# Step 2's transposes on TensorE and its feed-forward in one piece, with wider planning margins

## The chip, the cores and the metric

One core of one Trainium2 chip runs the whole program. The number to explain is the device time of one launch in microseconds (us). Before the change the median of three executions is 214.18 us (212.68 to 214.71). The execution that was profiled took 214.71 us. Its span in the trace is 213.0 us, and the 1.7 us around it are not in the trace.

## The reference, cut to what matters

A gated linear attention runs over 4 batches, 8 heads, 768 positions and a head size of 48. Its output, 3072 rows of 384, goes through a feed-forward with 1536 inner rows.

```python
f = 1.0 / (1.0 + np.exp(-f_logit))
for t in range(S):
    state = f[:, :, t, :, None] * state + np.einsum('bhd,bhe->bhde', k[:, :, t], v[:, :, t])
    y[:, :, t] = np.einsum('bhd,bhde->bhe', q[:, :, t], state)
...
x = np.ascontiguousarray(attn_out.transpose(0, 2, 1, 3)).reshape(B * S, H * D)
...
gate = np.maximum(x @ w_gate, 0.0)
val = x @ w_val
return (gate * val @ w_out).astype(np.float32)
```

## The kernel before, in words

**Steps.** The 768 positions are cut into six steps (`c` = 0 to 5) of 128 positions. In every step each of the four batches (`b`) goes through `attention(c, b)`, and then 512 rows (4 batches of 128) go through the feed-forward of that step.

**Attention of one batch in one step.** ScalarE takes the exponential and the logarithm of the gate's logits for two batches at once (L576, L579). TensorE adds the logarithms up along the positions (the cumulative sums, L586 and L588), ScalarE exponentiates the result (L595, L597), and GpSimd multiplies k and q by it (L606, L609, into `hats`). These are then transposed into `qkT`: in steps 0 and 1 by TensorE into PSUM (L619) and copied out by VectorE (L625), from step `first_xbar_qk` on by a transposing DMA that SyncE's queue issues (L628). TensorE forms the scores (L642), VectorE masks them into `ptm` (L648, two instructions for a batch), TensorE forms the output (L677, L681), and ScalarE copies it to `xn` (L695). The output is transposed once more into `xT`, by TensorE and VectorE in steps 1 and 2 (L703, L707) and by a transposing DMA from step 3 on (L711). The state for the next step is made by L722, L736 and L738.

**Feed-forward.** For each of 12 blocks `j` of 128 inner rows, `ffn_hidden` (L754) forms the gate and the value, each with three matmuls over the columns of the batches `b0` to `b1`. ScalarE applies the relu (L761), VectorE multiplies (L765, into `gT`). `ffn_out` (L776) then forms one batch's output with 12 matmuls of 384 columns, ScalarE copies it to `osb` (L788) and SyncE's queue stores it (L791). The list `groups` says how the batches of a step are taken together: an entry `(2,0,2,0)` is step 2, batches 0 and 1 together, so matmuls of 256 columns; `(4,0,4,0)` is all four batches at once with 512 columns. An entry needs the `xT` of all its batches.

**What sets the order.** Nothing is ordered at run time. `Plan.schedule` gives every operation an estimated start from fixed costs (`occ`, `lat`, for a DMA also `flow` and `late`), always takes the operation that could start earliest, and writes one fixed order for each engine; each engine then runs its order and waits on semaphores where an operand comes from elsewhere. The planner adds a margin to the estimated arrival of an operand: `pl.margin` for TensorE and SyncE, and `pl.more` on top for TensorE operations of the attention once the planned time is past `pl.later` (85.0). Feed-forward matmuls have a priority number from 1000 up, take no margin, and serve as filler. PSUM has eight banks: two for scores, four for the feed-forward, one each for the rest.

**SyncE's queue.** Loads of f, k, q and v (L398; 384 KB each, two batches), transposing DMAs and stores all stand in one queue in the planned order. A load waits until the load three places before it has landed (`flight = 3`), and a transposing DMA or store waits for the engine that makes its operand. Whatever stands behind waits too.

Of the kernel before, what the change touches and what calls it, by code (L numbers as in the profile page):

```python
# [43 lines left out]
class Plan:  # L44
# [9 lines left out]
    def add(self, eng, emit, reads=(), writes=(), occ=0.5, lat=0.2, prio=0, opens=(), after=(), follows=(),  # L54
            paced=()):
        op = Op(eng, emit, list(reads), list(writes), occ, lat, prio, opens, after, follows, paced)
        op.idx = len(self.ops)
        self.ops.append(op)
        return op
# [169 lines left out]
def bass_hgrn2_outer__then__ffn_reglu_kernel(  # L229
# [11 lines left out]
             "q0.2.3 q0.3.4 v0.2.3 v0.3.4 wg0 wv0 wg1 wv1 wg2 wv2 wg3 wv3 f1.0.2 k1.0.2 q1.0.2 v1.0.2 "  # L241
             "wo0 wo1 wo2 f1.2.4 k1.2.4 q1.2.4 v1.2.4").split()
    lag = 4.0
    first_xbar_qk = 2
    flight = 3
    WP = 0
    NWARM = 100
# [6 lines left out]
    first_xbar_x = 3  # L254
    load_batches = 2
    hat_engines = ['DVE', 'POOL']
    groups = [(0,0,4,1),(1,0,2,0),(1,2,4,0),(2,0,2,0),(2,2,4,0),(3,0,2,0),(3,2,4,0),(4,0,4,0),(5,0,4,0)]
    B, H, S, D = q.shape
    C = 128
    NC = S // C  # L260
# [12 lines left out]
    NL = 3  # L273
# [42 lines left out]

    pl = Plan({"bc": 1, "tp": 1, "s": 2, "y": 1, "kv": 1, "f": 4, "w": 1})
    pl.settled, pl.margin = 40.0, {"PE": 0.5, "SP": 0.6}
    pl.later, pl.more = 85.0, 0.5
    add = pl.add  # L320
    gp, ve, sc, te, sy = nc.gpsimd, nc.vector, nc.scalar, nc.tensor, nc.sync

# [51 lines left out]
    def dma(op, slot, flow, late=0.8):  # L374

        if slot not in slots:
            slots[slot] = [nc.alloc_semaphore(f"d_{slot}"), 0]
        slots[slot][1] += 16
        op.sem, op.goal = slots[slot]
        op.flow, op.late = flow, late  # L380
# [3 lines left out]
    def load(n, c, b0, b1, after=(), paced=(), eng="SP"):  # L384
        last = tails.get("load" + eng)
        e = sy if eng == "SP" else sc
        t = ld[n][c % NL]
        src = bass.AP(tensor=srcs[n].tensor, offset=b0 * H * S * D + c * C * D,
                      ap=[[D, C], [S * D, (b1 - b0) * H], [1, D]])
        dst = t[:, b0:b1, :, :].rearrange("p b h d -> p (b h) d")  # L390
        flow = 0.9 * (b1 - b0)
        if c == 0 and n != "v":
            u = b0 % 2
            src = bass.AP(tensor=srcs[n].tensor, offset=b0 * H * S * D, ap=[[2 * D, 64], [S * D, H], [1, 2 * D]])
            dst = t[64 * u:64 * u + 64, b0 - u:b0 - u + 2, :, :].rearrange("p b h d -> p (b h d)").rearrange(
                "p (h x) -> p h x", h=H)
            flow = 0.82
        op = add(eng, lambda: e.dma_start(dst, src), [], [f"{n}{c % NL}_{b}" for b in range(b0, b1)],  # L398
                 occ=(0.6 if eng == "SP" else 0.3) * (b1 - b0) * (0.8 if c == 0 else 1), lat=2.0 if c == 0 else 0.9, prio=c * 100 - 150 * (eng != "SP"), after=after,
                 follows=[last] if last else [], paced=paced)  # L400
        tails["load" + eng] = op
        dma(op, f"{n}{c % NL}_{b0}{b1}", flow, (6.0 if (c, n, b0) == (1, "v", 0) else 2.0 if c < 3 else 2.0) if c else 0.8)
        return op

    w_cuts = {"wg": [int(x) for x in ['0', '2', '4', '8', '12']], "wo": [0, 4, 8, 12]}
# [7 lines left out]
    def load_w(nm, s, after, landed=()):  # L413
        j0, j1 = w_cuts[nm][s:s + 2]
        if nm == "wo":
            src = bass.AP(tensor=w_out.tensor, offset=j0 * 128 * DM, ap=[[DM, 128], [128 * DM, j1 - j0], [1, DM]])
            dst = wo[:, j0:j1, :]
        else:
            src = bass.AP(tensor=wsrc[nm].tensor, offset=j0 * 128,
                          ap=[[DFF, 128], [128 * DFF, NK], [1, (j1 - j0) * 128]])  # L420
            dst = (wg if nm == "wg" else wv)[:, :, j0 * 128:j1 * 128]
        last = tails.get("load_w")
        op = add("POOL", lambda: gp.dma_start(dst, src), [], [f"{nm}{s}"], occ=0.8, lat=1.0, prio=WP, paced=after,
                 after=landed, follows=[last] if last else [])
        tails["load_w"] = op
        dma(op, f"{nm}{s}", 6.3 * (j1 - j0) / NJ)
        return op
# [4 lines left out]
    for item in early:  # L432
        weight = item[0] == "w"
        cost, need = 0.0, []
        for other, flow, op in reversed(done):
            if cost >= lag and other != weight:
                need = [op]
                break
            cost += flow
        if weight:  # L440
            landed = [first_of[wo_after[int(item[2:])]]] if item[:2] == "wo" else []
            op = load_w(item[:2], int(item[2:]), [] if landed else need, landed)
        else:
            c, b0, b1 = (int(x) for x in item[1:].split("."))
            op = load(item[0], c, b0, b1, need)
            if c == 1:
                first_of.setdefault(item[0], op)
        done.append((weight, op.flow, op))
# [9 lines left out]
    for i in range(NWARM):  # L458
        op = add("PE", lambda: te.matmul(cold.ap[:, 0:256], zeros[:, 0:128], zeros[:, :]), ["zeros"], [cold], occ=0.22 if i < NCOLD else 0.11,  # L459
                 lat=PE_L, prio=1000000, opens=[cold] if i == 0 else [])  # L460
# [342 lines left out]
    for c in range(NC):  # L803
        for b in range(0, B, load_batches):
            for n in "fkqv":
                if c > max(int(x.split(".")[0]) for x in sent):
                    if load_engine == "SP":
                        loads.append(load(n, c, b, b + load_batches, loads[-flight:][:1]))
                    else:
                        loads.append(load(n, c, b, b + load_batches, paced=loads[-flight:][:1], eng="ACT"))  # L810
        for b in range(B):
            attention(c, b)
        if c == 0 and split_first:
            for j0 in range(0, NJ, JB):
                for b0 in (0, 2):
                    for j in range(j0, j0 + JB):
                        ffn_hidden(0, b0, b0 + 2, j)
            for b in range(0, B, OPAIR):
                ffn_out(0, *range(b, b + OPAIR))
        for gc, b0, b1, now in groups:  # L820
            if gc != c or (c == 0 and split_first):
                continue
            for j in range(NJ):
                ffn_hidden(c, b0, b1, j)
                if pend and (NJ - 1 - j) * 1.0 / NJ * len0 < len(pend):
                    ffn_out(*pend.pop(0))
            mine = [(c, b) for b in range(b0, b1)]
            pend = pend + mine
            while now and pend:
                ffn_out(*pend.pop(0))  # L830
            len0 = len(pend)
# [6 lines left out]
    for e in ("PE", "ACT", "DVE", "POOL"):  # L838
        n = 0
# [72 lines left out]
```

## Time and profile before

| | |
|---|---|
| median of three executions | 214.18 us |
| profiled execution / its span | 214.71 us / 213.0 us |
| TensorE busy | 191.2 us (90%), clock at 0.998 |
| ScalarE, VectorE, GpSimd busy | 117.5, 106.6, 78.8 us |
| feed-forward matmuls of 256 columns (L754) | 576, in groups of three |
| feed-forward matmuls of 512 columns (L754) | 144, in groups of three |
| transposing DMAs for `qkT` / for `xT` | 16 / 12 |
| last load issued | 145.38 us from the start |

In the profile, a line such as L628 is a line of the kernel above. "PE" is TensorE's matmuls, "PEld" its weight loads, "DVE" VectorE, "ACT" ScalarE, "POOL" GpSimd, and "SPq" SyncE's queue. Matmuls are pipelined, so the duration that the profile gives for one is longer than the distance between two starts; distances are what adds up. A group of three 256-column matmuls takes 0.49 us by itself, but the next group starts 0.33 us later.

### The profile page before, as it was taken

The numbers are of one execution on the slowest core, as the hardware profiler recorded it, in microseconds if no ns is written. First come the engines' busy times: TensorE is split into PE (matmuls) and PEld (weight loads), VectorE is DVE, ScalarE is ACT, GpSimd is POOL, SyncE is SP. The second block draws the span as 40 slices with busy tenths as digits, with TensorE's granted clock in tenths as the row PEclk, the third lists the DMA queues.
The fourth block names the chain that finished last, engine by engine and source line by source line (L and its number), as shares of the span: only waits on it lengthen the run. The fifth ranks groups of instructions, "written<-read, shape, count | busy, mean of one in ns | idle before, by whom it ended". The sixth has DMA issues, their size and how long they took to land.

```text
span 213.0 us, 4826 instructions
## 1 busy us (share of the span) xinstructions
PE 191.2 (90%) x1903; PEld 134.3 (63%) x1903; DVE 106.6 (50%) x228; ACT 117.5 (55%) x287; POOL 78.8 (37%) x113
## 2 busy tenths in 40 slices
PE   7896999979999999959768678788999999999994
PEld 6685788756886877737555556555775454445562
DVE  7248966444694767544545445334582535233310
ACT  2976758527898775928428457084454434433411
POOL 5389103913879737465642433606100000000000
PEclk9999999999999999999999999999999999999999
DMA  5999999999999999999999799899922010111112
GB/s 128 233 217 180 202 201 200 221 205 246 253 190 196 202 170 243 188 198 187 144 207 202 144 223 133 172 218 181 209 59 74 0 42 0 37 37 37 40 42 107
DMA packets 123207, 32.83 MB, mean 154 GB/s; under 512 B 115504, under 2 KB 123184, under 8 KB 123184
## 3 DMA queue, kind: packets, MB, share of 16 engines
q1 hardware_dynamic: 118400, 28.98, 70.7%
q0 software_dynamic: 4784, 3.54, 11.1%
q8 instruction: 15, 0.25, 0.5%
q14 instruction: 8, 0.07, 0.2%
HBM read 25.95 MB, written 4.72 MB: 144 GB/s over the span
## 4 chain that ended last, share of the span: by engine, by line
PE 55%; DMA 19%; SPq 12%; ACT 7%; POOL 3%; issue 2%; DVE 1%
PE ps L754 30%; PE ps L776 16%; SPq L398 5%; DMA f_in<-in_f_logit_dram 5%; DMA qkT<-hats 5%; SPq L628 5%; DMA wo<-in_moe_w_out_dram 3%; DMA v_in<-in_v_dram 3%; DMA q_in<-in_q_dram 3%; ACT relu L761 2%; PE ps L642 2%; SPq L711 2%; PE ps L722 1%; ACT f_in L576 1%; ACT bneg L579 1%
## 5 line engine op out<-in xcount | busy, mean ns | idle before, releaser
L765 DVE TENSOR_TENSOR gT<-relu,ps 128x256 bf16<-128x256 bf16 (+1 forms) x120 | 54.3, 470 | 58.5 <-ACT relu L761 29.5
L754 PE MATMUL ps<-xT,wv 128*128 128x256 bf16 (+1 forms) x360 | 66.7, 294 | 2.1 <-ACT relu L761 1.2
L761 ACT ACTIVATE relu<-ps 128x256 bf16<-128x256 f32 (+1 forms) x120 | 49.9, 429 | 31.9 <-PE ps L754 31.1
L754 PE MATMUL ps<-xT,wg 128*128 128x256 bf16 (+1 forms) x360 | 66.6, 294 | 0.4 <-DVE xT L707 0.4
L776 PE MATMUL ps<-wo,gT 128*128 128x384 bf16 x288 | 52.4, 326 | 1.3 <-DMA wo<-in_moe_w_out_dram 1.3
L754 PEld LDWEIGHTS ps<-xT,wv 128*128 128x128 bf16 x360 | 33.3, 98 | 14.7 <-ACT relu L761 1.4
L754 PEld LDWEIGHTS ps<-xT,wg 128*128 128x128 bf16 x360 | 33.6, 98 | 12.2 <-DVE xT L707 0.7
L648 DVE TENSOR_TENSOR ptm<-ps,tri 128x512 bf16<-128x512 f32 x48 | 31.0, 684 | 17.3 <-PE ps L642 17.2
L776 PEld LDWEIGHTS ps<-wo,gT 128*128 128x128 bf16 x288 | 26.7, 98 | 17.7 <-DMA wo<-in_moe_w_out_dram 1.7
L788 ACT ACTIVATE osb<-ps 128x384 f32<-128x384 f32 x24 | 11.6, 489 | 30.3 <-PE ps L776 30.2
L606 POOL TENSOR_TENSOR hats<-k_in,expo 128x384 bf16<-128x384 f32 x20 | 19.9, 997 | 16.7 <-ACT expo L595 16.6
L609 POOL TENSOR_TENSOR hats<-q_in,expo 128x384 bf16<-128x384 f32 x20 | 20.0, 998 | 10.1 <-DMA q_in<-in_q_dram 8.0
L738 POOL TENSOR_TENSOR st<-ssum,dec 128x384 bf16<-128x384 f32 x16 | 13.3, 830 | 17.2 <-DVE ssum L736 17.2
L642 PE MATMUL ps<-qkT 48*128 48x128 bf16 x192 | 9.5, 218 | 7.8 <-DMA qkT<-hats 7.8
L562 POOL CAST vpad<-v_in 128x384 bf16<-128x384 f32 x24 | 11.9, 518 | 11.0 <-DMA v_in<-in_v_dram 10.3
L576 ACT ACTIVATE f_in<-f_in 128x768 f32<-128x768 f32 x10 | 8.4, 841 | 13.4 <-DMA f_in<-in_f_logit_dram 13.4
L459 PE MATMUL ps<-zeros 128*128 128x256 bf16 x91 | 12.8, 294 | 1.1 <-DVE zeros L358 1.1
L695 ACT ACTIVATE xn<-ps 128x384 bf16<-128x384 f32 x20 | 9.8, 488 | 6.2 <-PE ps L681 6.1
L642 PEld LDWEIGHTS ps<-qkT 48*128 48x128 bf16 x192 | 5.5, 94 | 11.9 <-issue 6.6
L736 DVE TENSOR_TENSOR ssum<-ps,st 128x384 f32<-128x384 f32 x16 | 8.9, 554 | 6.9 <-PE ps L722 6.8
L595 ACT ACTIVATE expo<-ps 128x384 f32<-128x384 f32 x20 | 9.9, 496 | 2.3 <-PE ps L588 2.0
L459 PEld LDWEIGHTS ps<-zeros 128*128 128x128 bf16 x91 | 9.2, 105 | 2.6 <-DVE zeros L358 1.1
(71 smaller groups left out, 152.6 us busy)
## 6 DMA issues: line engine op xcount, KB each, us to landing
out_dram<-osb SPq DMA_DIRECT2D x24, 192.0 KB, 2.4
f_in<-in_f_logit_dram SPq DMA_DIRECT2D x10, 384.0 KB, 5.1
k_in<-in_k_dram SPq DMA_DIRECT2D x10, 384.0 KB, 5.2
q_in<-in_q_dram SPq DMA_DIRECT2D x10, 384.0 KB, 5.4
v_in<-in_v_dram SPq DMA_DIRECT2D x10, 384.0 KB, 4.9
wo<-in_moe_w_out_dram POOLq DMA_DIRECT2D x3, 384.0 KB, 7.4
f_in<-in_f_logit_dram SPq DMA_DIRECT2D x4, 192.0 KB, 3.7
k_in<-in_k_dram SPq DMA_DIRECT2D x4, 192.0 KB, 4.2
```

Source lines behind the costliest of these rows:

```text
L459: op = add("PE", lambda: te.matmul(cold.ap[:, 0:256], zeros[:, 0:128], zeros[:, :]), ["zeros"], [cold], occ=0.22 if i < NCOLD else 0.11, l ...
L562: add("POOL", lambda: gp.tensor_copy(vout, vin[:, b, :, :].rearrange("p (n j) d -> p n j d", j=2)), [f"v{li}_{b}", f"vpad{vi}"], [f"v_{vi} ...
L606: add("POOL", lambda: gp.tensor_tensor(hk, kin[:, b, :, :], ex[:, 1, :].rearrange("p (h d) -> p h d", h=H), ALU.mult), [f"k{li}_{b}", f"ex ...
L609: add("POOL", lambda: gp.tensor_tensor(hq, qin[:, b, :, :], ex[:, 0, :].rearrange("p (h d) -> p h d", h=H), ALU.mult), [f"q{li}_{b}", f"ex ...
L642: mm = te.matmul(s.ap[:, p * C:(p + 1) * C], qkT[qi][lo:lo + D, 1, p, :], qkT[qi][lo:lo + D, 0, p, :])
L648: add("DVE", lambda j=j, s=s: ve.tensor_tensor(ptm[mi][:, j, :, :], s.ap[:, :].rearrange("p (n t) -> p n t", n=NP), mask, ALU.mult), [s, " ...
L738: add("POOL", lambda: gp.tensor_tensor(t4(s_new), t4(tmp), rate, ALU.mult), [key] + dk, [f"S{b}_{c % 2}"], prio=P + 8, **pool_t(HD))
L754: mm = te.matmul(bank.ap[:, 0:n], wt[:, kt, j * 128:(j + 1) * 128], xT[xi][:, kt, n0:n1], start=(kt == 0), stop=(kt == NK - 1))
L761: add("ACT", lambda: sc.activation(relu[ri][:, 0:n], gate.ap[:, 0:n], AF.Relu), [gate], [f"relu{ri}"], prio=P, **act_t(n))
L765: add("DVE", lambda: ve.tensor_tensor(gT[gi][:, j, n0:n1], relu[ri][:, 0:n], val.ap[:, 0:n], ALU.mult), [val, f"relu{ri}"], [f"gT{gi}_{j}_ ...
L776: mm = te.matmul(o.ap[:, 0:DM], gT[gi][:, j, b * C:(b + 1) * C], wo[:, j, :], start=(j == 0), stop=(j == NJ - 1))
L788: add("ACT", lambda o=o, oi=oi: sc.activation(osb[oi][:, :], o.ap[:, 0:DM], AF.Copy), [o], [f"osb{oi}"], prio=P, **act_t(DM))
```

## The change

Four values differ. In step 2, q and k are transposed by TensorE and copied by VectorE, as in step 1, in place of four transposing DMAs. Step 2's feed-forward takes all four batches together, so its hidden matmuls have 512 columns. The planner adds 1.0 instead of 0.5 to the arrival of operands of attention work on TensorE after its time 85, and it takes loads from step 3 on to land 1.0 later than it did. The last two values move instructions only, through the planner's order.

```diff
-    first_xbar_qk = 2
+    first_xbar_qk = 3
...
-    groups = [(0,0,4,1),(1,0,2,0),(1,2,4,0),(2,0,2,0),(2,2,4,0),(3,0,2,0),(3,2,4,0),(4,0,4,0),(5,0,4,0)]
+    groups = [(0,0,4,1),(1,0,2,0),(1,2,4,0),(2,0,4,0),(3,0,2,0),(3,2,4,0),(4,0,4,0),(5,0,4,0)]
...
-    pl.later, pl.more = 85.0, 0.5
+    pl.later, pl.more = 85.0, 1.0
...
-        dma(op, f"{n}{c % NL}_{b0}{b1}", flow, (6.0 if (c, n, b0) == (1, "v", 0) else 2.0 if c < 3 else 2.0) if c else 0.8)
+        dma(op, f"{n}{c % NL}_{b0}{b1}", flow, (6.0 if (c, n, b0) == (1, "v", 0) else 2.0 if c < 3 else 3.0) if c else 0.8)
```

## The prediction

> **What bounds the kernel now.** I read the busy times by stretch first, then TensorE's waits, then the order of TensorE and of SyncE's queue.
>
> ```profile
> core 0: us, PE busy (x) PEld busy (x) DVE busy (x) ACT busy (x) POOL busy (x), PEclk, DMA share, GB/s
> 64.00:85.00 21.00, 20.42 (x251) 15.85 (x248) 14.07 (x32) 14.64 (x41) 14.56 (x20) 1.00 1.16 203
> 85.00:150.00 65.00, 51.49 (x582) 38.15 (x579) 30.52 (x66) 36.08 (x97) 29.70 (x37) 1.00 1.05 185
> 150.00:211.00 61.00, 60.08 (x379) 33.12 (x377) 22.73 (x38) 24.52 (x47) 0.91 (x2) 1.00 0.18 52
> ```
>
> TensorE is full from 64 to 85 and from 150 to the end. Between 85 and 150 it idles 13.5 of 65 us, while the DMA share stands at 1.05.
>
> ```profile
> PE ps L642 <- DMA qkT<-hats: 7.8, 5, 2.6
> PE ps L722 <- POOL vpad L562: 2.1, 2, 1.2
> ```
>
> The largest wait is that of the scores (L642) for the transposing DMA; `vpad` waits for loads too. In TensorE's timeline the last such wait is that of step 5, batch 1:
>
> ```profile
> 146.55 0.36 PE L681 MATMUL ps<-vpad,ptm 128*128 128x48 bf16 x8
> 147.85 0.40 PE L642 MATMUL ps<-qkT 48*128 48x128 bf16 x8 [0.93 <-DMA qkT<-hats]
> 148.18 0.50 PE L754 MATMUL ps<-xT,wg 128*128 128x256 bf16 x3
> ```
>
> From 147.85 on nothing stops it until its last matmul, whose end starts the last copy (in the chain that ended last, "210.11 0.49 ACT osb L788"). SyncE's queue is what delivers late:
>
> ```profile
> 60.88 1.52 SPq L398 DMA_DIRECT2D q_in<-in_q_dram  x1
> 62.74 2.27 SPq L628 DMA_TRANSPOSE qkT<-hats  x1
> 65.06 0.58 SPq L398 DMA_DIRECT2D v_in<-in_v_dram  x1
> 65.68 3.40 SPq L628 DMA_TRANSPOSE qkT<-hats  x1
> 69.13 0.58 SPq L398 DMA_DIRECT2D f_in<-in_f_logit_dram  x1
> 69.75 1.85 SPq L398 DMA_DIRECT2D k_in<-in_k_dram  x1
> ...
> 82.96 2.88 SPq L628 DMA_TRANSPOSE qkT<-hats  x1
> 85.88 0.58 SPq L398 DMA_DIRECT2D q_in<-in_q_dram  x1
> ```
>
> A load behind loads takes some 1.75 us of the queue; a transposing DMA with the load behind it takes 3.3. From 62.74 to 85.88 the queue passes eight loads and five transposes in 23.1 us: (23.1 - 8 x 1.75)/5 = 1.8 us for each transpose. So two things bound the kernel: TensorE's own work, and in steps 3 to 5 a queue that feeds it late. The end is the latest, over all waits, of "operand there + TensorE work still behind it".
>
> **What the Trainium skill says.** "Advanced Engine Details and Errata", X-Bar Transpose (TRN2), holds transposing DMAs to be as fast as plain ones, 350 to 400 GB/s. One here reads 1,024 packets of 256 B, which would be 0.7 us at that rate (an estimate from the page); the trace says 1.8 us of the queue and 4.7 us (median) to landing, so I use the trace. "TensorE: Matmul & The Clock Gate", Part 4: PE-mode transpose, says that the result goes to PSUM and a DVE copy must follow. The trace agrees: eight at L619 in 0.45 us, then L625 with 683 ns. The same page, Back-to-back issue gap, gives nearly the same cost per column for 256 and 512 columns (isolated gap, 262 and 518 cycles). The trace agrees: three take 0.328 us apart at 256 (1.64 us for 15) and 0.648 at 512 (7.77 for 36).
>
> **The change part by part.**
>
> *Transposes of step 2.* Removed: four L628 from SyncE's queue between 62.7 and 78, 4 x 1.8 = 7.2 us. Added: 4 x 0.45 = 1.8 us on TensorE and 4 x 0.68 = 2.7 us on VectorE.
>
> *Feed-forward of step 2 in one piece.* 144 matmuls of 256 become 72 of 512: 24 x (2 x 0.328 - 0.648) = 0.2 us less TensorE. ScalarE saves 24 x 0.387 - 12 x 0.597 = 2.1 us and VectorE 24 x 0.416 - 12 x 0.687 = 1.7 us; neither is the bound, so that is taken at nothing: TensorE's matmuls cover it, and were the cover gone it would be worth at most those two figures. The price: its first matmul needs all four `xT`, where before it needed two (81.9 us).
>
> *TensorE's total.* I add up both planned orders from 63.85 us, where they part, with these distances: L642 x8 0.33, L677 and L681 together 0.37, L722 x4 0.17, L586 and L588 0.27, L703 x3 0.18, L776 x4 0.65. Unhindered, the old order would end at 192.1 and the new one at 194.3, so 2.2 us more (1.6 by parts and 0.6 by which group stands where at the cut). The old one really ended at 210.1: 18 us of holes, large and small.
>
> *Wider margins.* They cost no instruction; they put more feed-forward ahead of the scores. Summed in the two orders, TensorE work left from a score to the end is:
>
> - step 4, batch 3: 72.3 before, 72.3 after
> - step 5, batch 0: 65.2 before, 62.2 after
> - step 5, batch 1: 61.9 before, 57.3 after
> - step 5, batches 2 and 3: 55.3 and 53.7 before, 51.4 and 49.7 after
>
> That filler covers TensorE's wait. If each operand came at its old time, the new end would be max(134.67 + 72.3, 143.50 + 62.2, 147.85 + 57.3) = 207.0, 3.1 us less.
>
> *When will operands come?* The queue's loads move up by some 7 us up to the last one before step 3's first transpose (from 82.5 to about 75). But that transpose waits for `hats`, and those for a cumulative sum in TensorE's order. In the new order this sum starts at 76.7 unhindered (76.75 before). Adding ScalarE's logarithm ahead (0.6), 0.3 for the sum, the exponential 0.4, on GpSimd k 1.0, a state product 0.8 (the new order has it in between), q 1.0 and handovers of 1.0 to 1.5 gives 81.8 to 82.3, against 82.96 in the old trace. Of the 7 us, one remains, and the loads behind (q and v of batches 2 and 3, then step 4's f and k) are held back by that wait. As the queue has run dry by then, the transpose should take the shortest L628's 1.3 us rather than 2.88: the next entry goes 2.2 us earlier.
>
> From there to the transpose of step 5, batch 1, both orders have 17 loads and 9 transposes for `qkT`; the new one has one `xT` transpose (1.2) and two stores (0.4 each) more, 2.0 us. So that operand comes 0.2 us earlier, at 147.65; batch 0, with one store more, 1.8 earlier, at 141.7. Step 4, batch 3 has one load and one `xT` fewer ahead (about 3 us): 134.7 - 2.2 - 3 = 129.5.
>
> *Sum.* max(129.5 + 72.3, 141.7 + 62.2, 147.65 + 57.3) = max(201.8, 203.9, 205.0) = 205.0. With the 0.4 us by which the old trace exceeds the same sum (210.1 against 147.85 + 61.9), TensorE ends at 205.4, 4.7 us earlier. Against the profiled execution: 214.71 - 4.7 = **210.0 us**; 2.0% under the median of 214.18.
>
> *Unknown costs.* New is that in three places two scores of 0.33 us follow each other with only 0.9 to 1.3 us of other work between them (step 3, batches 2 and 3; step 4, 0 and 1; step 5, 2 and 3). The second needs the two score banks back, after two masks of 0.62 us and a handover: 0 to 0.9 us each, 2.7 at most. The first two lie ahead of a later wait, which swallows them, so I take 0; below nothing it can't be. VectorE in step 2: by distance (gT 0.33, `xT` 0.28, mask and `qkT` 0.62, state sum 0.48) the new order holds 18.3 us of work where TensorE takes 20; I take no delay, the other end is the slower rival. Extra xT and stores: 1.0 to 3.5 us, 2.0 taken.
>
> **Rivals.**
>
> *The queue keeps its lead.* If the operands come the whole 7.2 us earlier, from a drained DMA system, the latest is step 5, batch 0: 143.5 - 7.2 + 62.2 = 198.5, and batch 1, 2 us less of a lead, 142.65 + 57.3 = 200.0. With the 0.4: 9.7 us less, **205.0 us**. For it: a DMA share of 1.05 in this stretch. Against it: the wait for `hats` worked out above.
>
> *No measurable difference.* The lead is lost in the queue: with 3.5 us for extra entries and a transpose that takes 2.9 after all, step 5, batch 1 comes at 150.7 or so, and with two late pairs the end is 150.7 + 57.3 + 0.4 + 1.0 = 209.4: **214.0 us**. For it: SyncE waits some 17 us for other engines between 56 and 150, which the new order may not shorten.
>
> *Slower: step 2 runs dry.* Between 63.85 and 85.2 the only filler is step 1's second half. Step 2's four batches pass transposes, copy, score, two masks, output, `xn`, transpose, copy, each in TensorE's order, with 2.7 us more on VectorE, and its own feed-forward can't start before the fourth. If each batch loses 2 us, step 3's cumulative sum is 8 us late, step 3's first transpose stands at 90, all loads behind it wait, and every later operand is 8 us later: 205.4 + 8 = 213.4, **218.0 us**. It decides from 4.7 us of delay on (equal), and from 6.8 us on the kernel is over 1% slower. For it: VectorE at 18.3 of 20. Against it: in the new order each mask and copy has 1.4 to 2.8 us of TensorE work behind which it hides.
>
> **How the numbers follow.** One per cent is about what a measurement of this kernel can tell from no change. Chances: forecast 0.41, lead kept 0.14, no difference 0.19, dry 0.26. The forecast's own spread (206 to 214) leaves a part within 1%. Faster by over 1% 0.54, within 1% 0.20, slower by over 1% 0.26. The range, 204.5 to 218.0, takes in the lead kept and the dry case up to its worked value; the faster cases' own range is 204.5 to 212.
>
> **What would show it.** Right: no L628 before about 80 us; TensorE full until about 99 (step 3, batch 2); the waits of L642 for `qkT` fall mainly on step 4 and the sum of TensorE's holes drops from 18 to some 11 us; after step 5's second score no hole. Step 3's first transpose at 82 and the last load near 145 confirm the queue's part. Wrong: holes of TensorE between 64 and 90 with VectorE or ScalarE as releaser (dry), first transposes of step 3 before 79 (lead kept), or a last wait of L642 after 151.

## The result and the profile after

The changed kernel takes **205.76 us** in the median (205.38 to 206.17), the kernel before 213.89 us beside it: a ratio of **0.9625** (95% interval 0.9573 to 0.9676). The profiled execution took 205.67 us with a span of 203.9 us, so the step from the profile before is 9.0 us where 4.7 were worked out. The direction and the range held; the size is that of the rival "the queue keeps its lead" (205.0 us). Each set of runs below has its own runs of the kernel before on its chip (medians 213.8 to 216.2 us), so between sets only ratios compare. A few executions fell into a slower state; the ratios leave them out, and so do the two medians below where they would weigh (209.5 and 209.9 us).

Busy time by stretch after the change; columns as in the prediction's first fence.

```profile
64.00:85.00 21.00, 21.00 (x275) 16.92 (x273) 16.49 (x37) 15.82 (x42) 15.43 (x21) 1.00 1.04 205
85.00:150.00 65.00, 61.33 (x597) 39.35 (x596) 33.92 (x65) 38.76 (x95) 29.83 (x37) 0.97 1.01 190
```

TensorE idles 3.7 us between 85 and 150, before 13.5. Its waits, complete from 64 us on (total, times, longest):

```profile
PE ps L776 <- ACT osb L788: 2.9, 1, 2.9
PE ps L754 <- ACT osb L788: 0.8, 1, 0.8
```

None is for `qkT` or `vpad`, which were 7.8 and 2.1 us before. SyncE's queue around step 3's first transposing DMA and around that of step 5, batch 1:

```profile
76.72 1.40 SPq L398 DMA_DIRECT2D k_in<-in_k_dram  x1
80.28 1.34 SPq L628 DMA_TRANSPOSE qkT<-hats  x1
...
138.03 1.29 SPq L628 DMA_TRANSPOSE qkT<-hats  x1
139.37 0.58 SPq L398 DMA_DIRECT2D v_in<-in_v_dram  x1
```

Before, the same three stand at 82.96, 144.02 and 145.38. The first came 2.7 us earlier, the last two 6.0. TensorE's last matmul ends where the last copy starts, 9.0 us earlier than before (210.11):

```profile
201.08 0.49 ACT L788 ACTIVATE osb<-ps 128x384 f32<-128x384 f32 x1 [1.46 <-PE ps L776]
```

### The profile page after: what moved, and what is told of

Read it like the earlier page. It is cut to its first block, busy times and chain, and to the rows that moved or that the text cites. A ratio compares the mean times of both kernels' runs of the same rounds, so it can differ in the third digit from the quotient of the medians.

```text
span 203.9 us, 4705 instructions
## 1 busy us (share of the span) xinstructions
PE 192.6 (94%) x1863; PEld 129.4 (63%) x1863; DVE 108.1 (53%) x220; ACT 116.1 (57%) x275; POOL 78.6 (39%) x113
## 4 chain that ended last, share of the span: by engine, by line
PE 76%; DMA 11%; SPq 6%; ACT 3%; issue 2%; POOL 0%; DVE 0%
PE ps L754 41%; PE ps L776 20%; SPq L398 5%; DMA f_in<-in_f_logit_dram 5%; DMA wo<-in_moe_w_out_dram 4%; PE ps L642 3%; DMA q_in<-in_q_dram 3%; PE ps L722 2%; PE ps L586 2%; PE ps L681 2%; PE ps L677 1%; PE ps L619 1%; ACT relu L761 1%; SPq L711 1%; ACT osb L788 1%
## 5 line engine op out<-in xcount | busy, mean ns | idle before, releaser
L754 PE MATMUL ps<-xT,wv 128*128 128x256 bf16 (+1 forms) x324 | 64.5, 308 | 0.8 <-ACT osb L788 0.8
L754 PE MATMUL ps<-xT,wg 128*128 128x256 bf16 (+1 forms) x324 | 64.5, 308 | 0.0
L761 ACT ACTIVATE relu<-ps 128x256 bf16<-128x256 f32 (+1 forms) x108 | 48.1, 454 | 27.9 <-PE ps L754 27.2
L776 PE MATMUL ps<-wo,gT 128*128 128x384 bf16 x288 | 54.5, 333 | 4.3 <-ACT osb L788 2.9
L776 PEld LDWEIGHTS ps<-wo,gT 128*128 128x128 bf16 x288 | 27.0, 99 | 22.2 <-ACT osb L788 3.2
L754 PEld LDWEIGHTS ps<-xT,wv 128*128 128x128 bf16 x324 | 30.0, 98 | 14.8 <-ACT osb L788 1.0
L754 PEld LDWEIGHTS ps<-xT,wg 128*128 128x128 bf16 x324 | 30.0, 98 | 13.3
L595 ACT ACTIVATE expo<-ps 128x384 f32<-128x384 f32 x20 | 9.8, 489 | 5.4 <-PE ps L588 5.1
L576 ACT ACTIVATE f_in<-f_in 128x768 f32<-128x768 f32 x10 | 8.4, 841 | 7.4 <-DMA f_in<-in_f_logit_dram 7.4
L597 ACT ACTIVATE expo<-ps 128x384 f32<-128x384 f32 x20 | 9.9, 494 | 0.0
```

The source lines that it names most:

```text
L754: mm = te.matmul(bank.ap[:, 0:n], wt[:, kt, j * 128:(j + 1) * 128], xT[xi][:, kt, n0:n1], start=(kt == 0), stop=(kt == NK - 1))
L761: add("ACT", lambda: sc.activation(relu[ri][:, 0:n], gate.ap[:, 0:n], AF.Relu), [gate], [f"relu{ri}"], prio=P, **act_t(n))
L776: mm = te.matmul(o.ap[:, 0:DM], gT[gi][:, j, b * C:(b + 1) * C], wo[:, j, :], start=(j == 0), stop=(j == NJ - 1))
```

## Experiments: which part carries the gain

**Step 2's four transposing DMAs, taken out and put back.** The first kernel has all orders of the kernel before, without the four; the second has all orders of the kernel after, with four equal DMAs of a constant tile in their places.

```diff
+    gone = [op for op in order["SP"] if getattr(op, "ring", "") and op in step2]
+    for op in gone:
+        order["SP"].remove(op)
...
```

> The kernel before, all five orders as they were, but step 2's four transposing DMAs are left out of SyncE's queue and the scores of step 2 read what lies in their buffers, so part of the output is computed from old data. Only the queue is relieved; TensorE's order and margins stay. Theory Q (the four DMAs' 7.2 us in the queue are what the change gains): 205 to 208 us, TensorE's holes between 85 and 150 fall from 13.5 to under 7 us. Theory F (feed-forward placed ahead of the scores is what gains, the queue's lead is lost to the wait for hats): 211 to 213 us, step 3's first transpose near 82 and the last load near 144 as before.

```diff
+        op = Op("SP", lambda n=n: sy.dma_start(spare[n % 2].rearrange("p x n t -> p (x n) t"),
+                                               wo[:, 0:4, :].rearrange("p j m -> p (j m)")[:, 0:1024], transpose=True),
...
+        order["SP"].insert(order["SP"].index(near) + 1, op)
```

> The changed kernel, its orders as they are, with four transposing DMAs of the same shape put back into SyncE's queue at the places where step 2's stood before; they read a part of w_out and write a spare buffer that nobody reads. The queue carries the old load, TensorE's order and margins are the new ones. Theory Q: the gain goes, 211 to 214 us. Theory F: 205.5 to 208.5 us, with waits of the scores for qkT back in steps 4 and 5 but covered by the feed-forward ahead of them.

Measured: 206.14 us, ratio 0.9639 (0.9576 to 0.9702), without the four; 209.5 us, 0.978 (0.9711 to 0.9849), with four put back. The first is what theory Q expected; the second lies between the two theories. So the four cost 8.3 us in the old orders and 3 to 4 in the new ones, where more than half of the gain stays without the relief; the first kernel also lacks the 1.8 us that the changed kernel's TensorE spends on them. The queue of the first, at the same two places:

```profile
79.75 1.34 SPq L629 DMA_TRANSPOSE qkT<-hats  x1
...
135.38 1.31 SPq L629 DMA_TRANSPOSE qkT<-hats  x1
```

Step 3's first transpose comes only 3.2 us before its old time, step 5, batch 1's 8.6 us before. A wait for `hats` at the first (1.0 us) did not use the lead up.

**The parts alone.** First, `first_xbar_qk = 3` alone, and the two margins alone.

> Of the change only step 2's transposes on TensorE; feed-forward of step 2 in two pieces, margins as before. Theory Q: 206 to 208.5 us, most of the gain. Theory F: 211 to 214 us, for the added up order has 1.8 us more of TensorE work and no more filler ahead of the last scores (57.3 us left after step 5's batch 3, and 64.9 after batch 1).

> Of the change only the two planning margins; the four DMAs stay. Theory Q: 212 to 214 us. Theory F: 209.5 to 211.5 us: with operands at their old times the work left after step 5's batches 0 and 1 is 61.9 and 57.9 us, so TensorE ends at 143.50 + 61.9 or 147.85 + 57.9 and 0.4, 206.1 against 210.1.

Measured: 209.04 us, ratio 0.9769 (0.9705 to 0.9834), and 209.14 us, 0.9774 (0.9705 to 0.9842). The first lies just above theory Q's range, the second just below theory F's. Each gives some 5 us, all parts together 8.1: they overlap. Then each margin alone, and the changed kernel without its one-piece feed-forward, without both margins, and without the wider `pl.more`:

```diff
-    pl.later, pl.more = 85.0, 0.5
+    pl.later, pl.more = 85.0, 1.0
```

> The kernel before with one value changed: attention work on TensorE is planned 1.0 instead of 0.5 us behind its operands after the planner's time 85. If feed-forward put ahead of the scores is what matters, this alone gives most of what both margins gave: 209 to 211 us, with TensorE's waits for qkT at 4 to 6 us in place of 7.8. If the place of ScalarE's loads' work matters, it gives little: 212.5 to 215 us, with waits for qkT of 7 us and more.

```diff
-        dma(op, f"{n}{c % NL}_{b0}{b1}", flow, (6.0 if (c, n, b0) == (1, "v", 0) else 2.0 if c < 3 else 2.0) if c else 0.8)
+        dma(op, f"{n}{c % NL}_{b0}{b1}", flow, (6.0 if (c, n, b0) == (1, "v", 0) else 2.0 if c < 3 else 3.0) if c else 0.8)
```

> The kernel before with one value changed: loads from step 3 on are planned to land 1.0 us later. If what matters is that ScalarE's instructions which wait for a load stand further back in its order, this alone gives most of what both margins gave (5 us): 209 to 211 us, with the waits of L576 for f_in between 80 and 150 at 9 to 11 us in place of 13.4. If what matters is feed-forward put ahead of the scores, it gives little: 212.5 to 215 us, with L576 near 13 us.

> Step 2's transposes on TensorE and the wider margins, but step 2's feed-forward in two pieces of 256 columns as before. If the one-piece feed-forward is only a saving of TensorE time (0.2 us by the added-up matmuls) and the gain is made by the queue and the margins: 205.2 to 207 us, as the kernel after. Rival: the gathered feed-forward is what holds filler back for the stretch from 85 on, and without it the filler is used up before 85: 207.5 to 210 us, with waits of L642 for qkT of 3 us and more.

> Step 2's transposes on TensorE and its feed-forward in one piece, without the two wider margins. Step 2's transposes alone took 5 us off, all parts together 8.3. If the one-piece feed-forward and the margins do the same work (filler for the stretch from 85 on), this is near the kernel after: 205.5 to 207.5 us. If the margins work by where ScalarE stands at its loads, which one-piece feed-forward does not change: 208 to 210 us, with L576's waits at 8 us and more.

> The kernel after with attention work on TensorE again planned 0.5 behind its operands in place of 1.0. Since that value alone moved the kernel before by nothing measurable, it should give nothing here: 205 to 207 us. Rival: with the queue relieved the filler counts, and without it scores wait for qkT by 2 us and more: 207.5 to 209.5 us.

Measured: `pl.more` alone 213.34 us, ratio 0.9976 (0.9946 to 1.0007), nothing; the loads' margin alone **207.39 us**, 0.9698 (0.9632 to 0.9764), better than any expectation. I had taken `pl.more` for the value that puts feed-forward ahead of the scores. Added up with the prediction's distances, TensorE's work behind the score of step 5, batch 1 is 61.9 us in the kernel before and still 61.9 with the wider `pl.more`, but 56.4 with later loads: it is the loads' margin that puts feed-forward ahead. (ScalarE's waits for f fell too, from 13.4 to 5.9 us; the next section shows that in the kernel before they are worth next to nothing.) Without the one-piece feed-forward the changed kernel takes 206.23 us, 0.9639 (0.9568 to 0.971), as with it. Without both margins it takes 209.9 us, 0.9706 (0.9638 to 0.9774): 0.8 to 1.6% above the changed kernel's two ratios, as the second expectation had it, though the interval overlaps that of the first. Without the wider `pl.more` it takes 203.4 us, 0.9408 (0.9354 to 0.9462), faster than both expectations. That was repeated beside the changed kernel on one chip:

> The kernel after once more, beside no_more_again on one chip: a ratio to the kernel before of 0.957 to 0.968, as measured first.

> The kernel after with attention work on TensorE planned 0.5 behind its operands, once more: if the wider value costs the changed kernel some 2%, a ratio to the kernel before of 0.935 to 0.948, and 1.5 to 2.8% less than the kernel after on the same chip. If the difference was the chip's, 0.957 to 0.966.

Measured: the changed kernel 206.89 us, 0.9546 (0.9498 to 0.9595); with `pl.more` back at 0.5 **201.99 us**, 0.9332 (0.9294 to 0.937), which beats both kernels. Both ratios lie just below their ranges; the step between them, 2.4%, is the one expected. The stretch of the faster kernel from 85 on, and its waits for operands:

```profile
85.00:150.00 65.00, 63.46 (x610) 41.15 (x609) 34.64 (x65) 40.19 (x97) 29.84 (x37) 1.00 0.99 187
```

```profile
PE ps L642 <- DMA qkT<-hats: 1.3, 1, 1.3
PE ps L754 <- ACT relu L761: 0.2, 1, 0.2
```

Here only 53.7 us of work stand behind the score of step 5, batch 1, where the changed kernel has 57.3. Beside the later loads, the wider `pl.more` takes filler away from that place.

## Experiments: what sets the time of the operand

In the changed kernel the last stops of TensorE follow one chain: ScalarE stands at L576 for a late load of f, and the copy to `osb` that TensorE needs stands behind it. In the trace of the kernel after:

```profile
132.47 0.84 ACT L576 ACTIVATE f_in<-f_in 128x768 f32<-128x768 f32 x1 [4.37 <-DMA f_in<-in_f_logit_dram]
133.22 0.47 ACT L788 ACTIVATE osb<-ps 128x384 f32<-128x384 f32 x1
```

In all, ScalarE waited 13.4 us for f between 80 and 150 before, 7.4 after. My first theory was that this wait closes a loop: late load, late copies and `hats`, SyncE waiting for them, next load later. Two kernels take it away from the changed kernel: one puts step 5's L576 directly ahead of its logarithm L579, one puts step 5's loads of f directly behind the load of q ahead of them.

```diff
+    for op in [o for o in moved if o in act]:
+        log = next(o for o in act if op in o.deps)
+        act.remove(op)
+        act.insert(act.index(log), op)
...
```

> The kernel after, with one thing moved: the two exponentials of step 5's gate (L576), which wait for a late load, stand on ScalarE directly ahead of their logarithms, so behind the copies to osb that TensorE waited for (0.76 us at 119.71, 2.91 us at 133.74, and some 1.7 us at a lower clock after the second). If ScalarE's place in order is the last thing that stops TensorE, these holes go and nothing follows: 200.5 to 202.5 us, 3 to 5 less than the kernel after, TensorE's idle time from 85 to 150 under 1.5 us. Rival: the late load itself is the bound, so its wait turns up one stage later, at the cumulative sum or the scores of step 5: 204.5 to 206.5 us, with a wait of L586 or L642 in place of the one for osb.

```diff
+        spq.remove(op)
+        spq.insert(spq.index(q) + 1, op)
```

> The kernel after, with the two loads of step 5's logits put 6 to 7 us earlier in SyncE's queue, directly behind the load of q before them; all other orders are the same. If the late load is what is left of the holes (L576 waits 7.4 us in the kernel after, TensorE 3.7 us behind it and 1.7 us at a lower clock): L576 waits under 2 us, TensorE's idle time from 85 to 150 is under 1.5 us, and the kernel takes 201 to 203.5 us. Rival: what is moved ahead of pushes back as much (the transposes and v come later, or ScalarE waits for k's chain): 204.5 to 207 us with a new wait of TensorE for qkT or vpad.

Measured: 205.06 us, ratio 0.9586 (0.9519 to 0.9653), and 206.15 us, 0.9536 (0.9482 to 0.9591), against 0.9625 and 0.9546 for the changed kernel on two chips. Neither is a gain that can be told from nothing, and in both the wait came up elsewhere, as the rivals said (in the first at a place that its rival had not named):

```profile
PE ps L779 <- DVE gT L768: 3.1, 1, 3.1
PE ps L645 <- DMA qkT<-hats: 1.8, 3, 0.7
```

That is with ScalarE's order changed: now a relu behind L576 is late. With the earlier load ScalarE waits for f no more, and TensorE for `qkT` by 3.4 us. Next the wait was taken from the kernel before, with its orders and its loads kept:

```diff
-                add("ACT", lambda: sc.activation(fl, fl, AF.Exp, scale=-1.0), keys, keys, prio=P,
...
+                fs, fd = (wo[:, 0:2, :].rearrange("p j m -> p (j m)"), fb[:]) if c > 2 else (fl, fl)
+                op = add("ACT", lambda: sc.activation(fd, fs, AF.Exp, scale=-1.0), keys, keys, prio=P,
...
+        for d in [d for d in op.deps if d.sem is not None]:
+            del op.deps[d]
```

> The kernel before with all its orders and all its loads, but the gate of steps 3 to 5 is worked out from data that is already there (a slice of the output weights) and not from the loaded logits, so ScalarE's L576 of these steps waits for no load; the output is not the reference's. Before, these waits are 13.4 us. If the passage of SyncE's queue from step 3's first transposing DMA to that of step 5, batch 1 (61.1 us before, 57.8 after) holds waiting that comes from ScalarE standing at a late load, it falls to 56 to 58.5 us and the kernel takes 207 to 210 us. Rival, on which the prediction rests: the passage is the queue's own service time, so it stays at 60 to 61.5 us, the scores still wait for qkT, and the kernel takes 211.5 to 214 us.

> As f_free, and now the logarithm L579 doesn't wait for the loaded logits either (in f_free it took over 5.2 of the 13.4 us). ScalarE then waits for no load in steps 3 to 5. If ScalarE standing at late loads were a main cause of TensorE's holes, they fall from 13.5 us (85 to 150) to under 9 us and the kernel takes 207 to 210.5 us. If, as f_free says, they are not, the scores still wait for qkT by 7 us and more, and it takes 211.5 to 215 us, at a ratio to the kernel before of 0.99 to 1.00.

Measured: 215.2 us, ratio 0.9963 (0.9935 to 0.9991), and 214.83 us, 0.993 (0.9896 to 0.9963). In the first, L579 still waited 5.2 us for the load, so it took only a part away; in the second ScalarE waits for no load, and TensorE waits for `qkT` by 11.1 us. **The loop theory fell.** The second's queue is instructive:

```profile
86.36 2.97 SPq L635 DMA_TRANSPOSE qkT<-hats  x1
...
144.32 1.31 SPq L635 DMA_TRANSPOSE qkT<-hats  x1
```

The first transpose of step 3 starts 3.4 us later than in the kernel before, the last one shown only 0.3 us later. The passage between them did shrink (58.0 us in place of 61.1), and nothing came of it.

The loop also lacks a link: in this passage SyncE does not wait. The view of its waits names other engines for 14.6 us there, but a name in that view is an inference, and the operands had long been made. Here is the end of the passage in the kernel before, with the last piece of `hats` that the transpose at 144.02 reads:

```profile
134.70 0.99 POOL L609 TENSOR_TENSOR hats<-q_in,expo 128x384 bf16<-128x384 f32 x1
...
138.21 2.90 SPq L628 DMA_TRANSPOSE qkT<-hats  x1
141.15 0.58 SPq L398 DMA_DIRECT2D q_in<-in_q_dram  x1
141.78 2.20 SPq L711 DMA_TRANSPOSE xT<-xn  x1
144.02 1.31 SPq L628 DMA_TRANSPOSE qkT<-hats  x1
```

The operand was there 8.3 us before its turn. The same holds for every entry between 82.96 and 144.02: the instructions and loads that it depends on end before the entry ahead of it does, and each entry starts within 0.05 us of that one's end, but for one with 0.45 us between. So a late copy or late `hats` delayed nothing in this passage.

The other theory went by the entries. In both traces a transposing DMA directly behind a load takes 2.1 to 2.9 us of the queue, if the queue did not stand empty, and elsewhere mostly 1.3 (in the kernel before also 2.5 and 3.4); the nine of the passage take 25.2 us before and 18.1 after. So, in the kernel before, the seven that stand behind a load of k or q changed places with it:

```diff
+        if op.writes[0][0] in "kq" and op.writes[0][1] in "012" and t.writes[0][:3] == "qkT" and op.start > 70:
...
+            spq[n], spq[n + 1] = t, op
```

> The kernel before, with one thing moved: in SyncE's queue from 70 us on, each of the seven transposing DMAs for qkT that stands directly behind a load of k or q changes places with that load. In the kernel before the nine transposes of the passage from 82.96 to 144.02 take 2.80 us each, in the kernel after 2.02, and those that stand behind something other than a load take 1.3. If a transpose pays for the load directly ahead of it and this is what shortened the passage: transposes at 1.3 to 2.0 us each, the passage 57 to 59 us, the kernel 208 to 211.5 us. Rival: the bytes take their time wherever they stand, so the loads behind take what the transposes no longer do (loads above 1.1 us each in place of 0.74): passage 60 to 61.5 us and 212.5 to 214.5 us.

Measured: 215.47 us, ratio 0.9973 (0.9943 to 1.0003). The nine transposes do fall to 18.8 us in all, and loads and other entries take it back:

```profile
83.86 1.28 SPq L628 DMA_TRANSPOSE qkT<-hats  x1
...
144.02 1.31 SPq L628 DMA_TRANSPOSE qkT<-hats  x1
```

The passage is 60.2 us, and the transpose of step 5, batch 1 starts at 144.02 as before. The rival was right on the time, though not all of the balance sits in the loads: stores and `xT` transposes take 2.5 us more. Last, are bytes or entries what step 2's transposes cost?

```diff
-                op = add("SP", lambda: sy.dma_start(qkT[qi].rearrange("p x n t -> p (x n) t"),
...
+                nt = 3 if c == 2 else 8
+                op = add("SP", lambda: sy.dma_start(qkT[qi].rearrange("p x n t -> p (x n) t")[:, 0:nt, :],
...
```

> The kernel before with all its orders and all entries of SyncE's queue, but step 2's four transposing DMAs move three of the eight blocks of 128 columns (the scores of step 2 use what older steps left in the rest, so the output is not the reference's): 0.66 of 1.05 MB less. If what the change took away is bytes from a DMA system that moves some 190 GB/s whatever the order, it gives most of what leaving the four out gave: a ratio to the kernel before of 0.970 to 0.980. If it is the entries (their place and their issue in the queue), it gives under 1%: 0.992 to 1.000.

> before_less_t once more, beside small_t on one chip: a ratio to the kernel before of 0.955 to 0.970, as measured first (0.964), with step 5 batch 1's transposing DMA at 134 to 138 us.

Measured: 213.85 us, ratio 0.9939 (0.9905 to 0.9973), with small transposes; 209.18 us, 0.9683 (0.9611 to 0.9756), without them. Most of what the four cost goes with their entries in the queue, not with their bytes. With three eighths of the bytes they still hold the queue for 2.4 us each (2.7 before); each stands directly behind a load, and by the run with swapped entries a part of this time can be the load's:

```profile
63.45 2.56 SPq L629 DMA_TRANSPOSE qkT<-hats  x1
66.06 0.57 SPq L398 DMA_DIRECT2D v_in<-in_v_dram  x1
66.68 2.59 SPq L629 DMA_TRANSPOSE qkT<-hats  x1
```

The Trainium skill, "Perfetto Trace Analysis", What "DMA-bound" means, tells a bound by the issuing engine's sequencer, whose track is then solid with DMA instructions, from one by the DMA engines. Both signs are here: entries hold SyncE for 59.0 of the passage's 61.1 us, and the DMA share is 1.05 between 85 and 150. These runs favour the first: 0.6% for 0.66 MB of bytes, 3.2% for bytes and entries together. What sets the time of an entry, no run shows.

## Why the prediction was right in direction and wrong in size

**The sum held in every run in which the operand was waited for.** For each trace I took the landing of each transposing DMA for `qkT`, added the work behind its score, and kept the largest. In each it is that of step 5, batch 1. Times in us:

| kernel | ratio | transpose of step 5, batch 1 starts | lands | work behind its score | sum | TensorE's end |
|---|---|---|---|---|---|---|
| before | 1 | 144.02 | 147.81 | 61.9 | 209.7 | 210.1 |
| entries swapped with loads | 0.997 | 144.02 | 147.89 | 61.9 | 209.8 | 210.2 |
| no wait for f | 0.993 | 144.32 | 148.50 | 61.9 | 210.4 | 210.8 |
| small transposes | 0.994 | 142.91 | 146.95 | 61.9 | 208.8 | 209.2 |
| before without the four, two runs | 0.964, 0.968 | 135.38, 138.89 | 139.27, 142.85 | 61.9 | 201.1, 204.7 | 201.5, 205.1 |
| transposes on TensorE alone | 0.977 | 133.46 | 137.66 | 64.9 | 202.5 | 204.6 |
| loads' margin alone | 0.970 | 142.61 | 145.94 | 56.4 | 202.3 | 202.7 |
| `pl.more` alone | 0.998 | 140.03 | 146.05 | 61.9 | 208.0 | 208.5 |
| both margins alone | 0.977 | 142.58 | 145.88 | 57.9 | 203.8 | 204.3 |
| after with four put back | 0.978 | 142.26 | 146.84 | 57.3 | 204.1 | 204.6 |
| after, two runs | 0.963, 0.955 | 138.03, 139.92 | 141.29, 144.78 | 57.3 | 198.6, 202.1 | 201.0, 202.6 |
| after without one piece | 0.964 | 137.56 | 140.90 | 58.6 | 199.5 | 201.1 |
| after, `pl.more` 0.5, two runs | 0.941, 0.933 | 140.63, 140.17 | 143.84, 143.36 | 53.7 | 197.5, 197.1 | 198.0, 197.6 |

TensorE ends 0.4 to 0.5 us after the sum in all traces of the table but three. With the transposes on TensorE alone it is 2.1 us: TensorE's clock is at half from 138.26 to 141.67, just behind that score, and 3.41 us at half clock cost 1.7. In the first run of the changed kernel (2.5 us) and in the one without one piece (1.6) the operand did not set the end: it was there, and its score came later without a wait. The first and the second run of the changed kernel:

```profile
143.39 0.40 PE L642 MATMUL ps<-qkT 48*128 48x128 bf16 x8
144.92 0.40 PE L642 MATMUL ps<-qkT 48*128 48x128 bf16 x8 [0.40 <-DMA qkT<-hats]
```

In the first it is the pause for `osb` at 130.8 and the low clock behind it that made TensorE late.

**The step that failed** is the time of the operand: "But that transpose waits for `hats`" ... "Of the 7 us, one remains". It had the transpose of step 5, batch 1 start at 143.8 and land at 147.65, and made 205.4 of it for TensorE's end. Measured: start at 138.03 and 139.92, landing at 141.29 and 144.78. Two terms of that step were wrong.

- *The wait was sized too long.* It is there, 2.1 and 1.7 us, but it was to end at 81.8 to 82.3 and ended at 80.28 and 79.98. The cumulative sum did start when it was said to. But 0.6 us for the logarithm (L579) were added behind that start, though it ends ahead of it, and from the sum's start to the end of `hats` it took 3.8 us where parts of 3.5 and handovers of 1.0 to 1.5 were added:

```profile
74.76 0.84 ACT L579 ACTIVATE bneg<-f_in 128x768 bf16<-128x768 f32 x1
76.47 0.33 PE L586 MATMUL ps<-bneg,tri 128*128 128x384 bf16 x1
79.25 1.00 POOL L609 TENSOR_TENSOR hats<-q_in,expo 128x384 bf16<-128x384 f32 x1
```

  So the next entry came 4.2 and 4.5 us earlier than in the kernel before (81.67 and 81.38 against 85.88) and not 2.2.
- *Extra entries were added to the passage behind the wait.* From that next entry to the transpose of step 5, batch 1 the queue took 58.1 us before; with 2.0 us for one `xT` and two stores 60.1 were worked out; 56.4 and 58.5 were measured. SyncE hardly waits there (0.6 and 0.5 us, for `osb`), so the passage is the sum of its entries, but the time of an entry is not its own. From 80.28 to 138.03 the nine transposes take 7.1 us less than before, the 17 loads 2.8 more; eight `xT` take 14.2 us where seven took 14.4, seven stores 7.2 where five took 6.6.

In the first run these two are 2.0 and 3.8 us of the start, in the second 2.3 and 1.6. What sets the length of the passage in detail is not settled: counted from that next entry it is 53 to 59 us in all traces, and neither ScalarE's wait for f nor the place of the transposes does it alone. With the old orders and step 2's four entries in the queue, step 3's first transpose starts anywhere from 82.5 to 86.4, and step 5, batch 1's at 142.9 to 144.3. Without the four they stand at 79.4 to 79.8 and 135.4 to 138.9.

**The rival's time is in part luck.** Its lead is 7.2 us for the entries that left, less 2.0 for those that came, so 5.2; the operand started 6.0 us earlier than in the profile before, and in the second run 4.1 earlier than in that set's run with swapped entries. But the rival had no wait for `hats`, which took some 2 us, and in the first run TensorE ended later than its operand allowed. That the two made up for each other was not foreseen.

**Two readings of the lines were wrong.** Between 62.74 and 85.88 the queue passes seven loads, five transposes and two stores, not eight loads; with the stores' own 2.3 us a transpose still comes to 1.7 us. And "SyncE waits some 17 us for other engines" is what the view of waits says; between 56 and 150 only two entries had to wait for what they need, for 0.1 and 0.3 us.

**Right:** 7.2 us for the four entries (leaving them out gave 8.3 and 6.5 us); the work behind the scores, and that it decides; TensorE's total to within some 1.4 us (194.3, with 3.7 us of pauses and 1.7 of low clock, against 201.0); no L628 before about 80 us (80.28 and 79.98); VectorE in step 2, which delays nothing (TensorE is full from 64 to 85); pairs of scores at 0; the one-piece feed-forward as worth next to nothing. **Wrong beside the step above:** TensorE is full to 118.5 and not 99, the expected waits for `qkT` in step 4 do not occur in the first run (0.9 us in the second), the last load is issued at 139.37 and not near 145, and the margins were costed as one: the loads' margin carries all of their gain, `pl.more` none.

## What to carry to other kernels

Where several engines run fixed orders, the end can be read as the largest "operand's landing + work behind it" over the waits; here that held within 0.5 us in every trace in which the operand was waited for and the clock was full behind it, so a change is best judged by how it moves each of the two terms. A worked-out wait needs its handovers from a trace. A wait that a view reports needs one more look: find the end of the instruction that makes the operand; here 14.6 us of reported waits in one passage were none. Entries of a busy queue don't have a price of their own, so entries that come in can't simply be added. Two margins that look alike to a planner can do opposite things, so look at the order that each writes.

## What was not expected of the hardware

**The time that a transposing DMA holds the queue hardly follows its bytes.** Directly behind a load, at three eighths of the bytes, step 2's four held SyncE's queue for 2.14 to 2.59 us in place of 2.27 to 3.40; others of full size, behind other entries or an empty queue, held it for as little as 1.28 to 1.34 us.

**TensorE's clock after a short pause.** After the 2.9 us for `osb` the granted clock fell to half for 3.41 us, and twelve matmuls of L776 took 3.80 us; in the chain that ended last twelve take 1.95. The second run of the changed kernel shows the same. The pause's length alone does not decide. The pauses are 2.91 us in the changed kernel, 1.84 in the kernel without the four, 3.05 with ScalarE's order changed; here are stretches of 3.41 us around each of them, in this order (behind a stretch stand its length and TensorE's busy time; the third number from the end is the clock):

```profile
130.46:133.88 3.42, 0.51 (x5) 0.21 (x3) 0.00 (x0) 1.41 (x4) 0.43 (x1) 1.00 1.21 265
133.88:137.29 3.41, 3.41 (x12) 1.66 (x11) 1.17 (x3) 1.36 (x4) 0.00 (x0) 0.50 0.81 159
110.75:114.16 3.41, 1.57 (x29) 1.31 (x28) 0.89 (x3) 1.43 (x5) 2.90 (x3) 1.00 0.93 193
114.16:117.57 3.41, 3.41 (x20) 2.53 (x19) 2.22 (x5) 0.77 (x2) 0.95 (x2) 0.50 1.00 201
130.72:134.13 3.41, 1.99 (x15) 1.16 (x12) 0.00 (x0) 0.84 (x1) 1.21 (x2) 1.00 1.12 231
134.13:137.54 3.41, 1.77 (x19) 1.20 (x21) 0.75 (x2) 2.30 (x6) 0.00 (x0) 1.00 0.73 161
```

The stretches are not chosen freely. In each trace all changes of the clock lie whole multiples of 3.41 us apart (with the entries swapped, half clock begins at 86.84 and 134.62, 14 x 3.413 apart), so the clock can be read on a grid. In the 19 traces that recorded a change, from 9 us on, every grid stretch with TensorE busy for less than 44% of it was followed by half clock, none with more than 51% was; between the two both occur. The pause of 3.05 us lies across two stretches, busy for 58% and 52%. The Trainium skill, "TensorE: Matmul & The Clock Gate", Why this matters for your kernels, asks for no idle gaps above some 3 us; here a pause of 1.84 us cost the clock and one of 3.05 us did not.
